# Retention and a mixture of adapters on one Trainium2 core: the rounds of a software pipeline in another order

## The chip, the core and the metric

The kernel runs on one core of a Trainium2 chip. The metric is the device time of one execution in microseconds (us). The kernel before takes 183.67 us, the median of three runs (182.58 to 185.34).

## What is computed

All arrays are fp32. q, k and v have 8 batches, 8 heads, 576 positions and 64 columns. The core of the reference, cut:

```python
scores = scale * np.matmul(q, k.transpose(0, 1, 3, 2))
gamma = 1.0 - 2.0 ** (-5.0 - np.arange(H, dtype=np.float32))
Dmat = np.where(rel >= 0, gamma[:, None, None] ** rel[None, :, :], 0.0)
attn = np.matmul(scores * Dmat, v)                # rel = i - j
x = attn.transpose(0, 2, 1, 3).reshape(B * S, H * D)      # 4608 x 512
logits = x @ w_gate                               # 8 experts
# the two largest logits, softmax over these two: weights w
delta[mask] += w * ((x[mask] @ A[e]) @ B[e])      # rank 16
out = x + delta
```

## The kernel before, in words

A *unit* is 128 positions of two batches with all their heads, so that there are four units for each of the four full chunks; the 64 positions that are left of each sequence make two short units of four batches each. `seq` (lines 142 to 144) lists the 18 units: 14 full ones (chunks 0, 1, 2 and half of chunk 3), a short one, two full ones, a short one. A retention over chunks needs a state P for each pair of batches, in SBUF, that is decayed and added to from chunk to chunk.

The kernel writes out the order of every engine's instructions by hand (`manual_schedule`, line 136), so each engine's queue is in program order. The loop over t (line 745) makes one round for each unit u = unit t, and does in it the late parts of p1 = unit t-1 and p2 = unit t-2. The stages on TensorE, with their matmuls for a full unit, are:

- T, `stage_T` (line 232): transposes of q (16) and of k (16) into PSUM, each tile of 64 rows by 128 columns of the array. VectorE (DVE) scales and copies q to qT; ScalarE (ACT) copies k to kT. `transposes` (line 622) makes both for unit t+1 and then has GpSimd (POOL) scale v and swap its halves.
- S, `stage_S` (274): scores of k and q, 64 matmuls in 64x64 tiles, into four banks; `mask` (299), four DVE multiplications, copies them to rt.
- Q, `stage_Q` (313): the state P times qT, 32 matmuls in 64x64 tiles, into the two banks of px. There is none for chunk 0.
- U, `stage_U` (328): the state product of v and k, 32 matmuls of 128 rows by 64 columns, into the bank pu. `state` (336): DVE adds P to it (ACT copies it for chunk 0), POOL decays the sum into P.
- R1 and R0, `stage_R1` (346) and `stage_R0` (360): late and early half of the retention, added into px; 32 matmuls each, R1 in tiles of 128x64 and R0 in tiles of 64x64. R1 of a unit is done in its own round, R0 in the next one, then `copy_x` has ACT copy px to xT.
- Z, `stage_Z`: xT times the joint matrix AW of gate and A, 16 matmuls of the full array, into the bank pz. `route1`, `sig`, `route2` find the two best experts and scale z to zc (nine small DVE steps, a sigmoid on ACT).
- X, `stage_X` (520): two fp16 transposes of zc into the bank pzt; ACT copies it to zT.
- B, `stage_B` (530): x is transposed back into the two banks of po by 16 matmuls in tiles of 64x128. Y, `stage_Y` (549): zT times Bcat is added to it, 4 fp16 matmuls. `evac` (555) has ACT copy po to osb, and `store` (563) issues two DMAs of 256 KB each.

A short unit has `short_S` (64 matmuls), `short_mask`, `short_Q` and `short_R` (64 matmuls each) and no state. `short_Q` ends with a small copy `seen`, for which `short_R` waits.

PSUM has eight banks, numbered by the tag; a stage says which it takes. In the kernel before, po has banks 2 and 3 and the pairs (4, 5) and (6, 7) swap roles each round: one holds S's first half and then px, the other X and Z. S's second half, pu and pt_k are in 0 and 1. The order of a full round on TensorE is

    B(p2) R0(p1) S(u) X(p2) Z(p1) Y(p2) Q(u) U(u) R1(u) T(t+1)

All loads and stores are issued by SyncE (SP), the loads of unit t+4 at the start of round t, the store of p2 later in it. Two rounds differ: those of the short units, and that of the full unit after a short one. After the loop `last_Z` and `finish` (line 631) end the last two units.

Of the kernel before, what the change touches and what calls it, by code (L numbers as in the profile page):

```python
# [10 lines left out]
FP32 = mybir.dt.float32  # L11
# [7 lines left out]
def kernel(  # L19
# [384 lines left out]
    def short_Q(u, bk):  # L404
# [12 lines left out]


        w = mo.tile([128, 1], FP32, tag="see", name="see")
        u.seen = nc.scalar.copy(out=w, in_=u.px[1][:, HP - 1, 1, 63:64])  # L420
# [19 lines left out]
    def copy_x(u, shared=False):  # L440
        u.xT = []
        for s in range(2):
# [8 lines left out]
    def stage_Z(u, bk):  # L451
        u.pz = bank(bk, [128, 2, ER + E], "pz")
        for s in range(2):
            for dt in range(HP):
                mm(u.pz[:, s, :], u.xT[s][:, dt, :], AW[s][:, dt, :], dt == 0, dt == HP - 1)


    def last_Z(u, p):
        u.pz = []
        for s in range(2):  # L460
            pz = bank(6 + s, [128, ER + E], "pz")
# [3 lines left out]
            if s == 0:  # L465
                stage_Y(p)

    def last_B(u):
        u.po = [
            [bank(2 + 2 * s + cc, [128, HP, 64], f"po{cc}") for cc in range(2)]  # L470
# [15 lines left out]
    def route1(u):  # L486
        lg = mo.tile([128, 2, E], FP32, tag="lg", name="lg")
        m8 = mo.tile([128, 2, E], FP32, tag="m8", name="m8")
        ns = mo.tile([128, 2], FP32, tag="ns", name="ns")
        ar = mo.tile([128, 2, E], FP32, tag="ar", name="ar")  # L490
        ge = mo.tile([128, 2, E], FP32, tag="ge", name="ge")
        nc.vector.tensor_copy(out=lg, in_=u.pz[:, :, ER : ER + E])  # L492
        for s in range(2):
            nc.vector.max(out=m8[:, s, :], in_=lg[:, s, :])
        nc.vector.tensor_tensor(out=ns, in0=m8[:, :, 0], in1=m8[:, :, 1], op=ALU.add)
        nc.vector.scalar_tensor_tensor(
            out=ar, in0=lg, scalar=2.0, in1=ns.unsqueeze(2).broadcast_to((128, 2, E)),
            op0=ALU.mult, op1=ALU.subtract,
        )
        nc.vector.tensor_tensor(  # L500
            out=ge, in0=lg, in1=m8[:, :, 1:2].broadcast_to((128, 2, E)), op=ALU.is_ge
        )
        u.ar, u.ge = ar, ge

    def sig(u):
        u.sg = mo.tile([128, 2, E], FP32, tag="sg", name="sg")
        nc.scalar.activation(out=u.sg, in_=u.ar, func=AFT.Sigmoid)

    def route2(u):
        cm = mo.tile([128, 2, E], FP32, tag="cm", name="cm")  # L510
        nc.vector.tensor_tensor(out=cm, in0=u.ge, in1=u.sg, op=ALU.mult)
        u.zc = mo.tile([128, 2, ER], FP16, tag="zc", name="zc", bufs=4)
        nc.vector.tensor_tensor(
            out=u.zc.rearrange("p s (e r) -> p s e r", e=E),
            in0=u.pz[:, :, 0:ER].rearrange("p s (e r) -> p s e r", e=E),
            in1=cm.unsqueeze(3).broadcast_to((128, 2, E, R)),
            op=ALU.mult,
        )

    def stage_X(u, bk):  # L520
        pzt = bank(bk, [128, 2, 128], "pzt", FP16)
        u.zT = mo.tile([128, 2, 128], FP16, tag="zT", name="zT")
        for s in range(2):
            nc.tensor.matmul(  # L524
                pzt[:, s, :], lhsT=u.zc[:, s, :], rhs=ident16,
                is_transpose=True, start=True, stop=True,
            )
# [27 lines left out]
    def evac(u, ccs):  # L555

        for cc in ccs:
# [3 lines left out]
            nc.scalar.copy(out=bass.AP(o.tensor, o.offset, ap), in_=u.po[cc])  # L561
# [60 lines left out]
    def transposes(i, bq):  # L622
        u = get(i)
        if u:
            stage_T(u, "q", bq)
            stage_T(u, "k", (0, 1))
            scale_v(u)

    def finish(u, p):
        m8 = mo.tile([128, 2, E], FP32, tag="m8", name="m8")
        ns = mo.tile([128, 2], FP32, tag="ns", name="ns")
        sg = mo.tile([128, 2, E], FP32, tag="sg", name="sg")
        cm = mo.tile([128, 2, E], FP32, tag="cm", name="cm")
        zc = mo.tile([128, 2, ER], FP16, tag="zc", name="zc", bufs=4)
        zT = mo.tile([128, 2, 128], FP16, tag="zT", name="zT")
        u.osb = osp.tile([128, 2, HP, 2, 64], FP32, tag="osb", name="osb", bufs=4)

        for s in range(2):  # L640
            lg = u.pz[s][:, ER : ER + E]
            nc.vector.max(out=m8[:, s, :], in_=lg)
            nc.vector.scalar_tensor_tensor(
                out=ns[:, s : s + 1], in0=m8[:, s, 0:1], scalar=-1.0, in1=m8[:, s, 1:2],
                op0=ALU.mult, op1=ALU.subtract,
            )
            nc.scalar.activation(
                out=sg[:, s, :], in_=lg, func=AFT.Sigmoid, scale=2.0, bias=ns[:, s : s + 1]
            )
            if s == 0:  # L650
                evac(p, [0, 1])
                store(p)
            nc.vector.scalar_tensor_tensor(
                out=cm[:, s, :], in0=lg, scalar=m8[:, s, 1:2], in1=sg[:, s, :],
                op0=ALU.is_ge, op1=ALU.mult,
            )
            nc.vector.tensor_tensor(
                out=zc[:, s, :].rearrange("p (e r) -> p e r", e=E),
                in0=u.pz[s][:, 0:ER].rearrange("p (e r) -> p e r", e=E),
                in1=cm[:, s, :].unsqueeze(2).broadcast_to((128, E, R)),  # L660
                op=ALU.mult,
            )
        for s in range(2):
            pzt = bank(6 + s, [128, 128], "pzt", FP16)
            nc.tensor.matmul(
                pzt, lhsT=zc[:, s, :], rhs=ident16, is_transpose=True, start=True, stop=True
            )
            nc.scalar.copy(out=zT[:, s, :], in_=pzt)
            if s == 0:
                last_B(u)  # L670
        for s in range(2):
            for cc in range(2):
                mm(u.po[s][cc], zT[:, s, :], bv[:, :, cc ^ s, :], False, True)
            for cc in range(2):
                o = u.osb[:, s, :, cc ^ s, :]
                if cc:
                    nc.vector.tensor_copy(out=o, in_=u.po[s][cc])
                else:
                    nc.scalar.copy(out=o, in_=u.po[s][cc])
            b0 = 4 * u.x + 2 * s  # L680
            nc.sync.dma_start(
                out=out3[b0 : b0 + 2, 128 * u.c : 128 * u.c + LH, :].rearrange("n t d -> t n d"),
                in_=u.osb[:, s].rearrange("p a o d -> p (a o d)"),
            )
# [41 lines left out]
    stage_U(u1, 3)  # L726
    state(u1)
    stage_R1(u1)
    route2(u0)
    transposes(2, (4, 5))  # L730


    def adapters(p1, p2, bd, late):
        stage_X(p2, bd[0])
        stage_Z(p1, bd[1])
        route1(p1)
        stage_Y(p2)
        evac(p2, [0])
        sig(p1)
        route2(p1)  # L740
        if not late:
            evac(p2, [1])
            store(p2)

    for t in range(2, NU):
# [3 lines left out]
        u, p1, p2 = get(t), get(t - 1), get(t - 2)  # L749
        ba, be = (0, 1), (2, 3)  # L750
        bc, bd = ((4, 5), (6, 7)) if t % 2 == 0 else ((6, 7), (4, 5))
        last = t == NU - 1
        stage_B(p2, be)
        if u.full and p1.full:
            stage_R0(p1, None if get(t - 2).full else p1.seen)
            copy_x(p1)
            stage_S(u, bc + ba)
            mask(u)
            adapters(p1, p2, bd, False)

            stage_Q(u, bc)
            stage_U(u, ba[0])
            state(u)
            stage_R1(u)
        elif u.full:

            adapters(p1, p2, bd, False)
            stage_S(u, bc + ba)
            mask(u)
            stage_U(u, bd[0])  # L770
            stage_Q(u, bc)
            state(u)
            stage_R1(u)
            u.seen = nc.scalar.copy(out=warm, in_=u.px[1][:, HP - 1, 127:128])
        else:
            stage_R0(p1)
            copy_x(p1)
            short_S(u, ba)
            short_mask(u)
            if last:  # L780
                short_Q(u, bc)
            adapters(p1, p2, bd, last)
            if not last:
                short_Q(u, bc)
            short_R(u)
            copy_x(u, last)
        transposes(t + 1, bd)
# [3 lines left out]
    evac(p2, [1])  # L791
    store(p2)
    stage_B(p1, (0, 1))
    stage_X(p1, 4)
    last_Z(u, p1)
    finish(u, p1)
    return


# [28 lines left out]
```

## Time and profile before

| What | Value |
|---|---|
| median of three runs | 183.67 us |
| the profiled execution | 183.51 us |
| its span, first to last instruction | 181.8 us |
| granted TensorE clock, mean | 0.998 |
| DMA | 38.85 MB, 214 GB/s |

The span is what the trace sees; the profiled execution's own time lies 1.7 us above it. In the profile PE is TensorE's matmuls and PEld its weight loads. A row of a group reads: line, engine, operation, output<-input by the program's names, shapes, count, busy time, mean ns of one. The helper `mm` (line 265) records most matmuls, so many groups have L266 and are told apart by their tiles. Rows of the stretches below have busy us and number of instructions of each engine, the granted clock, the DMA engines' busy share and GB/s.

### The profile page before, as it was taken

What the parts mean: (1) busy time and instruction counts of PE and PEld (TensorE: products, weight loads), DVE (VectorE), ACT (ScalarE), POOL (GpSimd) and SP (SyncE); (2) the same over time, 40 slices, a digit from 0 to 9 for tenths busy, and PEclk for the clock granted to TensorE, in tenths of its full rate; (3) what the DMA queues carried; (4) which work ended last, traced back from release to release, by engine and by line L of the source; (5) the groups of instructions that cost most, each with busy time, mean ns of one, the idle gap of its engine ahead of it and who ended that gap; (6) DMA issues with size and microseconds to landing.
All of it is one profiled execution on the core that took longest, in us unless ns stands there. A gap on an engine that the chain in (4) does not pass through costs nothing.

```text
span 181.8 us, 10235 instructions
## 1 busy us (share of the span) xinstructions
PE 172.1 (95%) x4636; PEld 155.9 (86%) x4636; DVE 95.4 (52%) x269; ACT 73.5 (40%) x160; POOL 81.6 (45%) x102
## 2 busy tenths in 40 slices
PE   7989999999999999999999999999998999799980
PEld 2779899999898989899999999988897899689960
DVE  1175754745564746555555555564654455445440
ACT  3236154545252525252534343433433632325450
POOL 7466582836271809090908181727258006316000
PEclk9999999999999999999999999999999999999999
DMA  5999999979899998998998899878999999820053
GB/s 134 273 231 215 234 234 233 203 180 230 194 227 271 251 225 208 217 257 209 253 243 208 227 223 271 199 212 202 270 213 281 230 248 239 322 94 34 5 215 133
DMA packets 119035, 38.85 MB, mean 214 GB/s; under 512 B 114248, under 2 KB 114376, under 8 KB 118992
## 3 DMA queue, kind: packets, MB, share of 16 engines
q1 hardware_dynamic: 118688, 38.04, 84.1%
q8 instruction: 36, 0.59, 1.3%
q0 software_dynamic: 144, 0.13, 0.5%
q14 instruction: 7, 0.06, 0.1%
q10 hardware_dynamic: 160, 0.03, 0.1%
HBM read 28.88 MB, written 9.44 MB: 211 GB/s over the span
## 4 chain that ended last, share of the span: by engine, by line
PE 91%; DVE 3%; issue 2%; ACT 0%; DVEq 0%; ACTq 0%
PE px L266 23%; PE pz L266 19%; PE ps L266 12%; PE pu L266 9%; PE pt_q L240 6%; PE pt_k L240 5%; PE po L536 5%; PE po L266 4%; PE fill L266 3%; PE pzt L524 2%; PE ps_s L266 1%; DVE rt L305 1%; PE pa L266 1%; PE pl L266 1%; DVE qT L252 0%
## 5 line engine op out<-in xcount | busy, mean ns | idle before, releaser
L344 POOL TENSOR_TENSOR P<-pn,gdec 128x512 f32<-128x512 f32 x16 | 20.4, 1274 | 76.9 <-DVE pn L341 66.1
L305 DVE TENSOR_TENSOR rt<-ps,tri 128x384 f32<-128x384 f32 x64 | 31.3, 550 | 17.2 <-PE ps L266 17.2
L266 PE MATMUL pz<-AW,xT 128*128 128x136 f32 x288 | 37.8, 283 | 0.5 <-issue 0.5
L212 POOL TENSOR_TENSOR v<-v,pack 128x512 f32<-128x512 f32 x35 | 35.8, 1043 | 5.1 <-DMA v<-in_v_dram 5.0
L262 ACT COPY kT<-pt_k 128x512 f32<-128x512 f32 x36 | 19.3, 589 | 40.6 <-PE pt_k L240 40.6
L266 PEld LDWEIGHTS pz<-AW,xT 128*128 128x128 f32 x288 | 34.7, 190 | 0.9 <-issue 0.7
L252 DVE TENSOR_TENSOR qT<-pt_q,aqp 128x512 f32<-128x512 f32 x36 | 23.2, 686 | 23.1 <-PE pt_q L240 23.1
L561 ACT COPY osb<-po 128x512 f32<-128x512 f32 x34 | 19.5, 577 | 29.7 <-PE po L266 26.0
L266 PE MATMUL ps<-qT,kT 64*64 64x128 f32 (+1 forms) x1024 | 26.1, 247 | 1.7 <-issue 1.2
L266 PEld LDWEIGHTS ps<-qT,kT 64*64 64x64 f32 x1024 | 24.1, 133 | 2.8 <-issue 1.5
L266 PE MATMUL px<-rt,v 64*64 64x64 f32 (+1 forms) x512 | 21.5, 224 | 0.1
L266 PE MATMUL px<-rt,vs 64*64 64x64 f32 (+1 forms) x512 | 21.2, 223 | 0.0
L223 POOL COPY vs<-v 64x512 f32<-64x512 f32 x32 | 19.8, 618 | 1.7
L448 ACT COPY xT<-px 128x512 f32<-128x512 f32 x34 | 18.5, 593 | 3.4 <-PE px L266 2.6
L266 PEld LDWEIGHTS px<-rt,v 64*64 64x64 f32 (+1 forms) x512 | 17.8, 136 | 1.7 <-DVE rt L305 0.3
L266 PE MATMUL pu<-v,k 128*64 128x64 f32 x512 | 18.4, 225 | 0.1
L266 PEld LDWEIGHTS pu<-v,k 128*64 128x64 f32 x512 | 16.2, 138 | 2.7 <-issue 2.3
L266 PEld LDWEIGHTS px<-rt,vs 64*64 64x64 f32 (+1 forms) x512 | 17.6, 136 | 0.0
L266 PE MATMUL px<-qT,P 64*64 64x128 f32 (+1 forms) x512 | 15.6, 262 | 0.1
L266 PEld LDWEIGHTS px<-qT,P 64*64 64x64 f32 x512 | 12.5, 133 | 2.8 <-DVE lg L492 2.1
L341 DVE TENSOR_TENSOR pn<-pu,P 128x512 f32<-128x512 f32 x12 | 8.3, 691 | 9.1 <-PE pu L266 9.1
L240 PE MATMUL pt_q<-id,q 64*128 64x64 f32 x288 | 12.8, 229 | 0.0
(69 smaller groups left out, 164.7 us busy)
## 6 DMA issues: line engine op xcount, KB each, us to landing
q<-in_q_dram SPq DMA_DIRECT2D x36, 256.0 KB, 5.0
k<-in_k_dram SPq DMA_DIRECT2D x36, 256.0 KB, 4.5
v<-in_v_dram SPq DMA_DIRECT2D x36, 256.0 KB, 4.8
out_dram<-osb SPq DMA_DIRECT2D x36, 256.0 KB, 4.4
A<-in_moe_A_dram SPq DMA_DIRECT2D x1, 256.0 KB, 3.8
Bcat<-in_moe_B_dram POOLq DMA_DIRECT2D x1, 128.0 KB, 4.5
g<-c_g ACTq DMA_DIRECT2D x1, 20.0 KB
pack<-c_rest ACTq DMA_DIRECT2D x1, 10.0 KB, 2.9
```

The source lines that it names most:

```text
L212: eng.tensor_tensor(out=u.v[:, b * H : b * H + H, :], in0=u.v[:, b * H : b * H + H, :], in1=(gv if u.full else gvh).unsqueeze(2).broadcast ...
L223: nc.gpsimd.tensor_copy(out=vs[half(1 - r)], in_=u.v[half(r), H : 2 * H, :])
L240: nc.tensor.matmul(ps[r][:, hp, b, :], lhsT=src[sl, b * H + 2 * hp : b * H + 2 * hp + 2, :], rhs=id64[sl, :], is_transpose=True, start=Tru ...
L252: u.scaled = nc.vector.tensor_tensor(out=o, in0=ps[r], in1=aqp[:, :, a0 : a0 + 64].unsqueeze(2).broadcast_to((128, HP, 2, 64)), op=ALU.mult,)
L262: nc.scalar.copy(out=o, in_=ps[r])
L266: return nc.tensor.matmul(o, lhsT=l, rhs=r, start=start, stop=stop, skip_group_check=True)
L305: nc.vector.tensor_tensor(out=r.rearrange("p a s i -> p a (s i)"), in0=u.ps[ho][g].rearrange("p a s i -> p a (s i)"), in1=tri3.rearrange(" ...
L341: u.sum = nc.vector.tensor_tensor(out=flat(pn), in0=flat(u.pu), in1=flat(P[u.bp]), op=ALU.add)
L344: nc.gpsimd.tensor_tensor(out=flat(P[u.bp]), in0=flat(pn), in1=flat(gdec), op=ALU.mult)
L448: nc.scalar.copy(out=o, in_=u.px[s])
L536: nc.tensor.matmul(po[cc][:, s, dt, :], lhsT=u.xT[s][sl, dt, :], rhs=id64[sl, :], is_transpose=True, start=(dt == 0 and s == 0), stop=Fals ...
L561: nc.scalar.copy(out=bass.AP(o.tensor, o.offset, ap), in_=u.po[cc])
```

## The change

From t=5 on (`t > TURN`) a full round on TensorE is

    S(u) Z(p2) Y(p3) R0(p1) Q(u) T(t+1) B(p2) U(u) R1(u) X(p2)

so the adapters run one round later than before: Z in round t is that of unit t-2, and Y, evac and store are those of p3 = unit t-3. Rounds 2 and 3 keep the old order, round 4 has neither Z nor Y, and the end has more of them. Three pairs of banks turn: S's first half is in the pair a, which then takes Z (one bank for each half of pz) ; its second half is in c, which then takes px (in round 4, Q takes a instead); T writes to a[1], d[0] for q and d[1], a[0] for k, where d holds px of p1. U then takes a[1] and X takes d[0]. The three pairs then change roles. The routing is done half by half (eight DVE steps, two sigmoids). X is done in half columns, four matmuls in place of two, where it follows R1. The diff, cut to its core:

```diff
-    def stage_Z(u, bk):
-        u.pz = bank(bk, [128, 2, ER + E], "pz")
+    def stage_Z(u, bks, ss=(0, 1)):
+        if 0 in ss:
+            u.pz = []
+        for s in ss:
+            pz = bank(bks[s], [128, ER + E], "pz")
             for dt in range(HP):
                 mm(pz, u.xT[s][:, dt, :], AW[s][:, dt, :], dt == 0, dt == HP - 1)
             u.pz.append(pz)
...
+    def route(u):
...
+        def best(s):
+            nc.vector.max(out=m8[:, s, :], in_=lg[s])
+            nc.vector.scalar_tensor_tensor(
+                out=ns[:, s : s + 1], in0=m8[:, s, 0:1], scalar=-1.0, in1=m8[:, s, 1:2],
+                op0=ALU.mult, op1=ALU.subtract,
+            )
+            nc.scalar.activation(
+                out=sg[:, s, :], in_=lg[s], func=AFT.Sigmoid, scale=2.0, bias=ns[:, s : s + 1]
+            )
+
+        def times(s):
+            nc.vector.scalar_tensor_tensor(
+                out=cm[:, s, :], in0=lg[s], scalar=m8[:, s, 1:2], in1=sg[:, s, :],
+                op0=ALU.is_ge, op1=ALU.mult,
+            )
+            nc.vector.tensor_tensor(
...
         for s in range(2):
+            best(s)
+        for s in range(2):
+            times(s)
...
+    def stage_X(u, bk, cols=True):
...
+            for r in (half(0), half(1)) if cols else (slice(0, 128),):
+                nc.tensor.matmul(
+                    pzt[r, s, :], lhsT=u.zc[:, s, r], rhs=ident16,
+                    is_transpose=True, start=True, stop=True,
+                )
...
     stage_T(u1, "k", (0, 1))
+    stage_Z(u0, (2, 3))
     scale_v(u1)
...
-    stage_Z(u0, 2)
-    route1(u0)
-    sig(u0)
+    route(u0)
     stage_S(u1, (6, 7, 0, 1))
     mask(u1)
...
-    route2(u0)
-    transposes(2, (4, 5))
+    transposes(2, (4, 5), (0, 1))
...
+    TURN = 4
+    a, c, d, e = (0, 1), (4, 5), (6, 7), (2, 3)
     for t in range(2, NU):
...
+        u, p1, p2, p3 = get(t), get(t - 1), get(t - 2), get(t - 3)
         last = t == NU - 1
+        if t <= TURN:
+            stage_B(p2, e)
+            stage_R0(p1)
             copy_x(p1)
+        if t < TURN:
...
+        if u.full:
+            stage_S(u, a + c)
             mask(u)
+        else:
+            short_S(u, c)
+            short_mask(u)
+        if t > TURN:
+            stage_Z(p2, a)
+            route(p2)
+            stage_Y(p3)
+            evac(p3, [0])
+            if p1.full:
+                stage_R0(p1)
+                copy_x(p1)
+            evac(p3, [1])
+            store(p3)
+        if t == TURN:
+            stage_Q(u, a)
+            x, y, d = d, c, a
+        else:
+            if u.full:
+                stage_Q(u, c)
+            else:
+                short_Q(u, c, nc.vector.tensor_copy if last else nc.scalar.copy)
+            x, y, d = (a[1], d[0]), (d[1], a[0]), c
+        transposes(t + 1, x, y)
+        if last:
+            stage_X(p2, x[1])
+            short_R(u)
+            copy_x(u, True)
+        if t > TURN:
+            stage_B(p2, e)
+        if last:
+            stage_B(p1, a)
+            break
+        if u.full:
+            stage_U(u, x[0])
             state(u)
             stage_R1(u)
         else:
+            short_R(u)
+            copy_x(u, True)
+        stage_X(p2, x[1], u.full)
+        a, c = y, x
...
+    d0, d1 = x[1], y[0]
+    stage_Z(p1, (d1, c[0]))
+    route(p1)
+    stage_Y(p2)
+    evac(p2, [0, 1])
     store(p2)
+    stage_Z(u, (d0, c[1]), [0])
+    stage_X(p1, d1, False)
+    stage_Z(u, (d0, c[1]), [1])
+    route(u)
+    last_B(u, e + (c[0], d1))
...
+    last_X(0, nc.scalar.copy)
+    stage_Y(p1)
+    evac(p1, [0])
+    last_X(1, nc.vector.tensor_copy)
+    evac(p1, [1], nc.vector.tensor_copy)
+    store(p1)
...
```

The last unit's four products Y, its copies by ACT and DVE and its two stores follow as before.

More of the change, by code (lines that the diff above doesn't have):

```diff
@@ L402, in short_mask, with short_Q @@
             u.rt.append(r)
-    def short_Q(u, bk):
+    def short_Q(u, bk, copy=nc.scalar.copy):
         u.px = [bank(bk[s], [128, HP, 2, 64], f"px{s}") for s in range(2)]
@@ L419, in short_Q @@
         w = mo.tile([128, 1], FP32, tag="see", name="see")
-        u.seen = nc.scalar.copy(out=w, in_=u.px[1][:, HP - 1, 1, 63:64])
+        u.seen = copy(out=w, in_=u.px[1][:, HP - 1, 1, 63:64])
     def short_R(u):
@@ L437, in short_R, with copy_x @@
                             first = False
-    def copy_x(u, shared=False):
-        u.xT = []
-        for s in range(2):
+    def copy_x(u, shared=False, ss=(0, 1)):
+        if 0 in ss:
+            u.xT = []
+        for s in ss:
             xt = mo.tile([128, HP, 128], FP32, tag="xT", name="xT", bufs=8)
@@ L449, in copy_x @@
             u.xT.append(xt)
-    def stage_Z(u, bk):
-        u.pz = bank(bk, [128, 2, ER + E], "pz")
[L453 to L461, printed above, removed]
+    def stage_Z(u, bks, ss=(0, 1)):
+        if 0 in ss:
+            u.pz = []
+        for s in ss:
+            pz = bank(bks[s], [128, ER + E], "pz")
             for dt in range(HP):
@@ L464, in last_Z, with last_B @@
             u.pz.append(pz)
-            if s == 0:
-                stage_Y(p)
-    def last_B(u):
+    def last_B(u, bks):
         u.po = [
-            [bank(2 + 2 * s + cc, [128, HP, 64], f"po{cc}") for cc in range(2)]
+            [bank(bks[2 * s + cc], [128, HP, 64], f"po{cc}") for cc in range(2)]
             for s in range(2)
@@ L484, in last_B @@
                     )
-    def route1(u):
-        lg = mo.tile([128, 2, E], FP32, tag="lg", name="lg")
+    def route(u):
         m8 = mo.tile([128, 2, E], FP32, tag="m8", name="m8")
         ns = mo.tile([128, 2], FP32, tag="ns", name="ns")
-        ar = mo.tile([128, 2, E], FP32, tag="ar", name="ar")
-        ge = mo.tile([128, 2, E], FP32, tag="ge", name="ge")
-        nc.vector.tensor_copy(out=lg, in_=u.pz[:, :, ER : ER + E])
-        for s in range(2):
[L494 to L518, printed above, removed]
@@ L520, in stage_X @@
-    def stage_X(u, bk):
+        sg = mo.tile([128, 2, E], FP32, tag="sg", name="sg")
+        cm = mo.tile([128, 2, E], FP32, tag="cm", name="cm")
+        u.zc = mo.tile([128, 2, ER], FP16, tag="zc", name="zc", bufs=4)
+        lg = [u.pz[s][:, ER : ER + E] for s in range(2)]
+        def best(s):
[7 more added lines that the diff above has]
+            )
@@ new lines, in times @@
+        def times(s):
[4 more added lines that the diff above has]
+            nc.vector.tensor_tensor(
+                out=u.zc[:, s, :].rearrange("p (e r) -> p e r", e=E),
+                in0=u.pz[s][:, 0:ER].rearrange("p (e r) -> p e r", e=E),
+                in1=cm[:, s, :].unsqueeze(2).broadcast_to((128, E, R)),
+                op=ALU.mult,
+            )
@@ L523, in stage_X @@
         for s in range(2):
[L524 to L527, printed above, removed]
+            for r in (half(0), half(1)) if cols else (slice(0, 128),):
+                nc.tensor.matmul(
+                    pzt[r, s, :], lhsT=u.zc[:, s, r], rhs=ident16,
+                    is_transpose=True, start=True, stop=True,
+                )
         nc.scalar.copy(out=u.zT, in_=pzt)
@@ L553, in stage_Y, with evac @@
         u.osb = osp.tile([128, 2, HP, 2, 64], FP32, tag="osb", name="osb", bufs=4)
-    def evac(u, ccs):
+    def evac(u, ccs, copy=nc.scalar.copy):
         for cc in ccs:
@@ L560, in evac @@
             ap[1][0] += -64 if cc else 64
-            nc.scalar.copy(out=bass.AP(o.tensor, o.offset, ap), in_=u.po[cc])
+            copy(out=bass.AP(o.tensor, o.offset, ap), in_=u.po[cc])
     def store(u):
@@ L620, in get, with transposes @@
         return G.get(i)
-    def transposes(i, bq):
+    def transposes(i, bq, bk):
         u = get(i)
@@ L625, in transposes @@
             stage_T(u, "q", bq)
-            stage_T(u, "k", (0, 1))
+            stage_T(u, "k", bk)
             scale_v(u)
[L631 to L684, printed above, removed]
@@ L725 @@
     stage_Q(u1, (6, 7))
-    stage_U(u1, 3)
+    stage_U(u1, 4)
     state(u1)
     stage_R1(u1)
-    route2(u0)
-    transposes(2, (4, 5))
[L733 to L743, printed above, removed]
+    transposes(2, (4, 5), (0, 1))
+    TURN = 4
+    a, c, d, e = (0, 1), (4, 5), (6, 7), (2, 3)
     for t in range(2, NU):
@@ L748 @@
             G[t + 4] = make(t + 4)
-        u, p1, p2 = get(t), get(t - 1), get(t - 2)
-        ba, be = (0, 1), (2, 3)
-        bc, bd = ((4, 5), (6, 7)) if t % 2 == 0 else ((6, 7), (4, 5))
+        u, p1, p2, p3 = get(t), get(t - 1), get(t - 2), get(t - 3)
         last = t == NU - 1
-        stage_B(p2, be)
-        if u.full and p1.full:
-            stage_R0(p1, None if get(t - 2).full else p1.seen)
+        if t <= TURN:
+            stage_B(p2, e)
+            stage_R0(p1)
             copy_x(p1)
-            stage_S(u, bc + ba)
+        if t < TURN:
+            stage_S(u, c + a)
@@ L758 @@
             mask(u)
-            adapters(p1, p2, bd, False)
-            stage_Q(u, bc)
-            stage_U(u, ba[0])
+            stage_X(p2, d[0], False)
+            stage_Z(p1, (d[1], c[1]))
+            route(p1)
+            stage_Y(p2)
+            evac(p2, [0, 1])
+            store(p2)
+            stage_Q(u, c)
+            stage_U(u, a[0])
             state(u)
             stage_R1(u)
-        elif u.full:
-            adapters(p1, p2, bd, False)
-            stage_S(u, bc + ba)
-            mask(u)
-            stage_U(u, bd[0])
-            stage_Q(u, bc)
+            transposes(t + 1, d, a)
@@ new lines @@
+            c, d = d, c
+            continue
+        if u.full:
+            stage_S(u, a + c)
+            mask(u)
+        else:
[16 more added lines that the diff above has]
+            if u.full:
+                stage_Q(u, c)
+            else:
+                short_Q(u, c, nc.vector.tensor_copy if last else nc.scalar.copy)
+            x, y, d = (a[1], d[0]), (d[1], a[0]), c
@@ L772 @@
+        transposes(t + 1, x, y)
[10 more added lines that the diff above has]
+            stage_U(u, x[0])
             state(u)
             stage_R1(u)
-            u.seen = nc.scalar.copy(out=warm, in_=u.px[1][:, HP - 1, 127:128])
         else:
-            stage_R0(p1)
-            copy_x(p1)
-            short_S(u, ba)
@@ L779 @@
[L779 to L784, printed above, removed]
             short_R(u)
-            copy_x(u, last)
-        transposes(t + 1, bd)
+            copy_x(u, True)
+        stage_X(p2, x[1], u.full)
+        a, c = y, x
     u, p1, p2 = get(NU - 1), get(NU - 2), get(NU - 3)
-    evac(p2, [1])
-    store(p2)
-    stage_B(p1, (0, 1))
-    stage_X(p1, 4)
-    last_Z(u, p1)
@@ L796, with last_X @@
-    finish(u, p1)
+    d0, d1 = x[1], y[0]
+    stage_Z(p1, (d1, c[0]))
+    route(p1)
+    stage_Y(p2)
+    evac(p2, [0, 1])
+    store(p2)
+    stage_Z(u, (d0, c[1]), [0])
[3 more added lines that the diff above has]
+    last_B(u, e + (c[0], d1))
+    zT = mo.tile([128, 2, 128], FP16, tag="zT", name="zT")
+    def last_X(s, copy):
+        pzt = bank((d0, c[1])[s], [128, 128], "pzt", FP16)
+        nc.tensor.matmul(
+            pzt, lhsT=u.zc[:, s, :], rhs=ident16, is_transpose=True, start=True, stop=True
+        )
+        copy(out=zT[:, s, :], in_=pzt)
@@ new lines @@
+    last_X(0, nc.scalar.copy)
[4 more added lines that the diff above has]
+    store(p1)
+    u.osb = osp.tile([128, 2, HP, 2, 64], FP32, tag="osb", name="osb", bufs=4)
+    for s in range(2):
+        for cc in range(2):
+            mm(u.po[s][cc], zT[:, s, :], bv[:, :, cc ^ s, :], False, True)
+        for cc in range(2):
+            o = u.osb[:, s, :, cc ^ s, :]
+            if cc:
+                nc.vector.tensor_copy(out=o, in_=u.po[s][cc])
+            else:
+                nc.scalar.copy(out=o, in_=u.po[s][cc])
+        b0 = 4 * u.x + 2 * s
+        nc.sync.dma_start(
+            out=out3[b0 : b0 + 2, 128 * u.c : 128 * u.c + LH, :].rearrange("n t d -> t n d"),
+            in_=u.osb[:, s].rearrange("p a o d -> p (a o d)"),
+        )
```

## The prediction

> **What bounds the kernel now.** I read the page first: parts 1 and 4 say that TensorE is busy nearly all the time and carries the chain that ended last.
>
> ```profile
> PE 172.1 (95%) x4636; PEld 155.9 (86%) x4636; DVE 95.4 (52%) x269; ACT 73.5 (40%) x160; POOL 81.6 (45%) x102
> ```
> ```profile
> PE 91%; DVE 3%; issue 2%; ACT 0%; DVEq 0%; ACTq 0%
> ```
>
> A busy PE can still be a PE that waits, so I cut one steady round (t=8) at the first matmul of each stage. In order: S, X, Z, Y, Q, U, R1, both transposes T, B, R0.
>
> ```profile
> core 0: us, PE busy (x) PEld busy (x) DVE busy (x) ACT busy (x) POOL busy (x), PEclk, DMA share, GB/s
> 79.47:80.97 1.50, 1.50 (x76) 1.43 (x69) 0.54 (x2) 1.22 (x3) 1.44 (x3) 1.00 1.09 246
> 80.97:81.09 0.12, 0.12 (x8) 0.12 (x3) 0.12 (x2) 0.00 (x0) 0.12 (x1) 1.00 1.27 335
> 81.10:83.00 1.90, 1.90 (x18) 1.89 (x17) 1.28 (x3) 0.37 (x1) 0.84 (x2) 1.00 1.08 344
> 83.00:83.53 0.53, 0.53 (x6) 0.29 (x3) 0.29 (x3) 0.00 (x0) 0.00 (x0) 1.00 1.17 259
> 83.53:84.57 1.04, 1.04 (x34) 0.86 (x33) 0.71 (x6) 1.00 (x3) 0.00 (x0) 1.00 1.04 244
> 84.57:85.55 0.98, 0.98 (x36) 0.98 (x34) 0.43 (x2) 0.27 (x1) 0.00 (x0) 1.00 0.18 41
> 85.55:86.58 1.03, 1.03 (x38) 0.96 (x34) 0.69 (x1) 0.00 (x0) 0.00 (x0) 1.00 0.80 186
> 86.58:87.64 1.06, 1.06 (x36) 1.06 (x34) 0.30 (x1) 0.00 (x0) 0.96 (x1) 1.00 0.83 183
> 87.64:88.24 0.60, 0.60 (x22) 0.53 (x18) 0.60 (x2) 0.40 (x1) 0.60 (x2) 1.00 1.15 262
> 88.24:88.77 0.53, 0.53 (x36) 0.53 (x33) 0.38 (x1) 0.53 (x2) 0.53 (x1) 1.00 0.86 193
> ```
>
> The reader sees no gap: 9.30 us per round, and rounds 8 to 11 all take 9.30. No new order can win by hiding waits there; it can only change what lies between stages. The losses are elsewhere. The timeline shows stalls of 0.1 to 0.2 us in S at t=3 to 7, 0.18 and 0.53 at t=12, 0.74 and 0.50 at t=14, 1.6 at t=16 and 0.3 at t=17. The chain of waits at t=16:
>
> ```profile
> 154.49 1.27 PE ps L266 x53
> 155.76 1.22 issue
> 156.97 0.55 PE ps L266 x9
> ```
>
> Nothing that the program waits for stands there. Counting PE's records (loads, matmuls and its semaphore instructions), the stalls at 125.4, 138.4, 157.0 and 166.4 us all come at number 193 or 194 modulo 256, and the 36 packets of the instruction queue have 16 KB each. They are refills of the instruction stream: from a packet's start to the next block's first instruction 2.2 to 2.6 us pass when PE waits. All stalls at this remainder sum to 3.9 us; without them the span is 177.9.
>
> **What the Trainium skill says.** "Runtime: NRT & Kernel Launch", Instruction fetch mechanics: instructions come in 16 KiB blocks of 256, and a crossing is "mostly hidden". The trace has the blocks but not the hiding. "TensorEngine Tiling (Array Packing)", Key Properties: changing the tiling mode drains the engine. The trace agrees: the 16 matmuls of q's transpose right after R1 (another mode) take 0.55, those of k's after them 0.51; B before R0 (another mode) takes 0.60 against 0.50. A change costs 0.10 ahead of it and up to 0.05 after it. "PSUM — Partial Sum Buffer", PSUM bank collisions: guard by bank, so a matmul into a bank waits for its last reader; the new bank table is read by that rule.
>
> **The change, part by part.** Mode changes first. Old: S-X, Y-Q, Q-U, R1-T, B-R0. New: S-Z, Y-R0, Q-T, B-U, X-S. Five each, so the new order saves none.
>
> *Regular full round (t=5 to 13, 16).* S 1.50, then Z into the first bank of S, which waits for the first mask. The mask starts 0.96 after S and takes 0.55, 0.05 to be seen: 1.57 instead of 1.50. Z right after a change 1.91+0.05=1.96. Y 0.53, R0 0.53, Q 1.03 (0.98 if it gains from no longer following a change; R0 ahead of it is of its own mode), T 1.06, B 0.60, U 0.98. R1 loses the change behind it: 0.93. X as four half-column matmuls: not in the old trace; between 0.12 (free beside R1) and 0.35 (four of the 0.067 steps of the old pair, then 0.15 to leave); I take 0.07+0.15=0.22. Sum 9.41, +0.11 (between 9.26 and 9.6 with these ends).
>
> The shorter routing, eight small DVE steps and two sigmoids for nine steps and one, lies under PE's work (DVE is busy 0.52 of the span) and costs nothing there; it counts where zc is waited for, below.
>
> Covers in that round: q's transposes need the bank of copy_x (ACT order sig, sig, evac, copy, copy, evac): from Y's start ACT ends the first copy_x about 0.06 before T_q, the second 0.1 before T_k, the second evac 0.13 before B. DVE's zc is ready at 5.2, T_q starts at 5.6. All fit, none with room: if ACT is late, PE waits. POOL: scale_v and swap of t+1 (3.3 us) now stand before the P update, which is next needed four rounds on. SP: the store moves one round later, so from unit 9 on loads pass two more DMAs (about 1.3 us of queue earlier).
>
> *Prologue.* route(u0) has its last steps before mask(u1) on DVE. From pz at 18.90: 0.21+0.28+0.30+0.26+0.29 (steps of the old tail's chain) = 20.24, against 19.94: +0.3. t=2 therefore starts at 24.13. t=2 and 3 keep their order, 8.26 and 8.40: 40.79.
>
> *t=4.* B 0.60, R0 0.53, then S; Q takes S's first two banks and waits for two masks, 2.00 from S's start. Q 1.03, T 0.55+0.60, U waits for qT out of its bank: T_q's start +0.75+0.69+0.06=1.50, 0.35 late; U 0.98, R1 0.93, X 0.22. Sum 7.79: 48.58. Its Z and Y are paid at the end. Nine rounds: 133.27.
>
> *t=14 (short).* short_S takes the bank of X, just issued: X to zT copied is 0.75 in the old trace, so it starts 0.6 late. 0.60+1.29+1.96+0.53+0.53+1.09+1.06+0.60+1.09+0.22=8.97: 142.24. The old wait on `seen` (0.50) is gone, covered by T and B. *t=15:* no R0, so T waits 0.15 for zc: 9.03. *t=16:* 9.41: 160.68.
>
> *End, from there (t=17).* B of this round goes behind short_R. short_S late again, 0.60+1.29=1.89, Z 1.96, Y 0.53, R0 0.53, Q to short_R 1.59 (the old 0.65 wait on `seen` stays, X within it), short_R 1.09, two B 1.15, Z 1.96, Y 0.44, half Z 0.93, X late by 0.35 and 0.12, half Z 0.93: 13.5. Then a chain: pz seen 0.35 after its last matmul, routing 1.37, X, zT on DVE, evac of p1 on DVE 0.68, done at 16.5. SP then issues four stores (0.34, 0.43, 0.55, 0.55 in the old tail), the last at 17.95; from its issue to the end of the program the old trace has 3.89. Sum 21.84: span 182.5 without refills. Old: 3.9 of 181.8 are refills. For the new I take 2.6, fewer because its own waits (about 3 us) give the fetch time; 128 matmuls take between 3.6 and 5.6 us in both orders, so they don't vanish: 0.5 to 5. Span 185.1. The profiled run took 183.51, 1.7 over its span, and the median is 183.67: I add 1.7 and get 186.8.
>
> **Rivals.** *Refills fall into waits* (0.5 instead of 2.6): 184.7, not slower as far as a measurement can tell. For it: rounds 8 to 11 lost nothing. Against it: the dense stretch (R1, X, S) is as short as the old (B, R0, S). It decides once the new order's refills stay under 1 us. *ACT becomes the bound of the regular round:* the margins above are 0.06 to 0.13; with ACT 0.3 late PE loses 0.2 in each of ten rounds: 188.8. For it: five copies in a row; against it: each length is from a row. *Loads late:* T now comes some 4 us earlier against DMA, which carries 38 MB at a share near 1. k of unit 5 is issued by 40.0 and lands 3.9 to 5.6 later, T_k is due at 45.5: at worst some 1 us there and at t=5: 187.8. *The order does save:* X is free, Z and the masks cost nothing (9.2 a round), refills 0.5, t=4 without its waits: 182.5-2.1-1.0+0.5+1.7, about 181.6; with the tail 2 us better, under 180.
>
> **How the numbers follow.** My case 0.55 (its own range 185.2 to 188.4), refills 0.18, ACT 0.16, loads 0.07, saving 0.04. The range 183.8 to 189.6 leaves out the saving and the outer halves of the refill and ACT cases. Two per cent, about what a measurement of this kernel can tell from no change, is 180.0 to 187.3: a third of my case, the ACT case and the loads give slower 0.40; faster 0.04; within 0.56.
>
> **What would show it.** Regular rounds of 9.4 with Z about 1.57 after S; `ps_s` twice 0.6 late behind ACT's zT; Q at t=4 waiting for rt; idle PE without a releaser only at the 194th of 256 instructions; the last store 18 us after the last short_S was due. Rounds at 9.3 or below, or a tail under 20 us, would prove the costs wrong; rounds over 9.6, the margins.

## The result, and the profile after

The changed kernel takes 190.14 us (median of 6 runs, 188.62 to 194.11) against 184.84 (6 runs, 182.58 to 188.24, the three of above among them) for the kernel before: ratio 1.0347, 95% interval 1.0244 to 1.0451. Ratios and intervals compare only the faster executions of each kernel, those within 1.5% of its fastest, while medians are of all. It is slower, as the forecast leaned, but by twice as much (186.8 is 1.7% over the 183.67 that the forecast started from), and outside the range (183.8 to 189.6). The profiled execution took 190.78 us, its span is 189.1; the span's difference to before is 7.3 us.

Parts 1 and 4 of the page after. TensorE's share has hardly moved, but the chain now holds DVE at 6% and ACT at 3%, where they had 3 and 0:

```profile
PE 176.2 (93%) x4662; PEld 157.1 (83%) x4662; DVE 102.7 (54%) x273; ACT 74.5 (39%) x172; POOL 82.0 (43%) x102
```
```profile
PE 85%; DVE 6%; issue 3%; ACT 3%; DVEq 0%; ACTq 0%
```

A regular round of the new order without a stall, cut like the old one; in order S, Z, Y, R0, Q, both T, B, U, R1, X:

```profile
100.92:102.50 1.58, 1.57 (x69) 1.43 (x65) 0.61 (x2) 0.37 (x1) 1.58 (x2) 1.00 0.98 224
102.50:104.45 1.95, 1.95 (x16) 1.94 (x17) 1.66 (x5) 0.14 (x1) 1.89 (x3) 1.00 1.05 240
104.45:104.98 0.53, 0.53 (x6) 0.29 (x3) 0.29 (x3) 0.13 (x1) 0.49 (x2) 1.00 1.24 272
104.98:105.50 0.52, 0.52 (x33) 0.52 (x36) 0.49 (x4) 0.38 (x2) 0.52 (x1) 1.00 1.18 261
105.50:106.49 0.99, 0.99 (x46) 0.82 (x38) 0.44 (x2) 0.99 (x3) 0.01 (x1) 1.00 0.56 128
106.49:107.54 1.05, 1.05 (x36) 1.05 (x34) 0.30 (x1) 0.84 (x2) 0.00 (x0) 1.00 1.21 341
107.54:108.15 0.61, 0.61 (x23) 0.54 (x19) 0.61 (x2) 0.41 (x1) 0.00 (x0) 1.00 1.04 350
108.15:109.13 0.98, 0.98 (x35) 0.98 (x34) 0.38 (x1) 0.67 (x2) 0.00 (x0) 1.00 0.99 219
109.13:110.06 0.93, 0.93 (x38) 0.93 (x36) 0.64 (x1) 0.00 (x0) 0.00 (x0) 1.00 1.20 265
110.06:110.28 0.22, 0.22 (x11) 0.13 (x7) 0.05 (x1) 0.00 (x0) 0.02 (x1) 1.00 1.30 284
```

This is t=10. It takes 9.35 us, against 9.30 before and 9.41 forecast; from S to Z pass 1.58, and X takes 0.22. But only two of the rounds t=5 to 13 (t=5 is the other) are that clean. The nine took 89.6 us, 5.4 more than nine times 9.35. Two kinds of gaps fill the difference.

**The first kind is a refill**, as before. The chain of waits at t=8, S broken off seven matmuls before its end:

```profile
79.89 1.43 PE ps L266 x57
81.33 1.34 issue
82.67 0.34 PE ps L266 x7
```

Counted in all traces in one way (from one matmul's start to the next, where that is over 0.13 us and takes in a record 191 to 197 modulo 256, less 0.06), refills cost 3.8 us before and 5.1 after.

**The second kind was not foreseen.** The timeline of t=7 on all engines, lines on the path alone:

```profile
start us, us, engine line op out<-in xcount [idle before <-releaser]
...
73.43 0.17 DVE L492 MAX8 m<-pz 128x8 f32<-128x8 f32 x1 [0.54 <-PE pz L266]
73.61 1.04 POOL L212 TENSOR_TENSOR v<-v,pack 128x512 f32<-128x512 f32 x1 [2.46 <-DMA v<-in_v_dram]
73.64 1.02 DVE L493 SCALAR_TENSOR_TENSOR ns<-m 128x1 f32<-128x1 f32 x1
...
74.76 0.27 ACT L497 ACTIVATE sg<-pz,ns 128x8 f32<-128x8 f32 x1 [1.49 <-DVE ns L493]
...
74.93 0.58 ACT L561 COPY osb<-po 128x512 f32<-128x512 f32 x1
...
75.32 0.29 DVE L506 TENSOR_TENSOR zc<-pz,cm 128x128 f16<-128x128 f32 x1
75.39 1.09 ACT L449 COPY xT<-px 128x512 f32<-128x512 f32 x2
...
75.71 0.24 PE L240 MATMUL pt_q<-id,q 64*128 64x64 f32 x1 [0.38 <-issue]
```

`ns` is one element per partition and takes 0.16 us. Here it takes 1.02 and ends when POOL's v-scaling ends, which began 0.03 earlier. Behind it come, on DVE, the rest of the routing up to zc, and on ACT, in order, the sigmoid, the evac and the two copies of px. T of q needs the bank of Z's second half, which zc reads last, and then a bank of px, which ACT's first copy reads: from one matmul's start to the next 0.65 and then 0.33 us pass, where the clean round has 0.20 at the first of these places and no gap at the second. The groups of `ns`, before and then after:

```profile
L495 DVE TENSOR_TENSOR ns<-m 128x2 f32<-128x2 f32 x17 | 3.1, 180 | 0.6
```
```profile
L493 DVE SCALAR_TENSOR_TENSOR ns<-m 128x1 f32<-128x1 f32 x36 | 10.4, 288 | 1.2
```

The mean of 288 ns is made of values from 0.16 to 0.25 us and of eight from 0.42 to 1.02; most of T's late starts (t=7, 8, 11, 14) follow one of the eight. Before, `ns` was no smaller a risk by its operands, but in the regular rounds POOL was idle then. (In the prologue it was held there too: 0.35 us in this trace, 0.87 in a second one.) Round t=8 before, POOL and `ns`:

```profile
78.61 2.04 POOL L212 TENSOR_TENSOR v<-v,pack 128x512 f32<-128x512 f32 x2
80.72 1.26 POOL L223 COPY vs<-v 64x512 f32<-64x512 f32 x2
83.68 0.16 DVE L495 TENSOR_TENSOR ns<-m 128x2 f32<-128x2 f32 x1
86.68 1.27 POOL L344 TENSOR_TENSOR P<-pn,gdec 128x512 f32<-128x512 f32 x1 [4.70 <-DVE pn L341]
```

There the scaling follows T at the round's end and is over at 82, 1.7 us before `ns`. In the new order T is earlier, the scaling waits for v, and it falls on the routing. The waits of POOL for v (us in sum, times, longest), before and then after:

```profile
POOL v L212 <- DMA v<-in_v_dram: 5.0, 4, 2.3
```
```profile
POOL v L212 <- DMA v<-in_v_dram: 24.1, 12, 3.5
```

The Trainium skill has the mechanism ("SBUF — State Buffer", Who interferes with whom: a DVE instruction with two SBUF inputs contends with a GpSimd instruction that reads SBUF). `ns` reads m8 twice, and this trace agrees; `cm`, with one SBUF tensor and one in PSUM, keeps 0.21 to 0.23 us throughout.

### The profile page after: what moved, and what is told of

Its sections match the earlier page's. It is cut to its first block, busy times and chain, and to the rows that moved or that the text cites. A ratio compares the mean times of both kernels' runs of the same rounds, so it can differ in the third digit from the quotient of the medians.

```text
span 189.1 us, 10292 instructions
## 1 busy us (share of the span) xinstructions
PE 176.2 (93%) x4662; PEld 157.1 (83%) x4662; DVE 102.7 (54%) x273; ACT 74.5 (39%) x172; POOL 82.0 (43%) x102
## 4 chain that ended last, share of the span: by engine, by line
PE 85%; DVE 6%; issue 3%; ACT 3%; DVEq 0%; ACTq 0%
PE pz L266 19%; PE px L266 19%; PE ps L266 12%; PE pu L266 9%; PE pt_q L240 6%; PE po L536 5%; PE pt_k L240 4%; PE po L266 3%; PE fill L266 3%; DVE ns L493 2%; PE pzt L524 1%; DVE rt L305 1%; PE ps_s L266 1%; ACT osb L561 1%; ACT xT L449 1%
## 5 line engine op out<-in xcount | busy, mean ns | idle before, releaser
L497 ACT ACTIVATE sg<-pz,ns 128x8 f32<-128x8 f32 x36 | 9.6, 268 | 58.4 <-DVE ns L493 54.1
L266 PE MATMUL ps<-qT,kT 64*64 64x128 f32 (+1 forms) x1024 | 26.9, 248 | 3.0 <-issue 2.5
L266 PE MATMUL px<-rt,v 64*64 64x64 f32 (+1 forms) x512 | 22.1, 224 | 0.2
L528 ACT COPY zT<-pzt 128x256 f16<-128x256 f16 x17 | 6.4, 375 | 22.1 <-PE pzt L524 22.1
L240 PE MATMUL pt_q<-id,q 64*128 64x64 f32 x288 | 14.1, 229 | 1.1 <-issue 0.4
```

The costliest lines, as they stand in the source:

```text
L240: nc.tensor.matmul(ps[r][:, hp, b, :], lhsT=src[sl, b * H + 2 * hp : b * H + 2 * hp + 2, :], rhs=id64[sl, :], is_transpose=True, start=Tru ...
L266: return nc.tensor.matmul(o, lhsT=l, rhs=r, start=start, stop=stop, skip_group_check=True)
L497: nc.scalar.activation(out=sg[:, s, :], in_=lg[s], func=AFT.Sigmoid, scale=2.0, bias=ns[:, s : s + 1])
```

## Experiments

Theory A: the blocked `ns` is a cause of its own. Theory B: only TensorE's structure (order, end) costs, and A's stalls merely take the place of refills. Theory C: refills stop TensorE because the fetch stands in a DMA queue behind loads. Theory D, formed later: where the 256-record blocks end in the round decides how much.

**1. `ns` with one tensor input** (changed kernel; value unchanged).

```diff
-            nc.vector.scalar_tensor_tensor(
-                out=ns[:, s : s + 1], in0=m8[:, s, 0:1], scalar=-1.0, in1=m8[:, s, 1:2],
+            nc.vector.tensor_scalar(
+                out=ns[:, s : s + 1], in0=m8[:, s, 0:1], scalar1=-1.0, scalar2=m8[:, s, 1:2],
```

> The changed kernel, in which the small step ns = -(m0+m1) is a tensor_scalar with the second maximum as a per-partition scalar, so that it has one tensor input in SBUF instead of two. Theory A (POOL's scaling of v now runs at the time of the routing and blocks ns, which makes ACT's sigmoid, evac and copy_x late, and so TensorE's transposes): ns takes 0.2 us everywhere also while POOL works (up to 1.0 us in the changed kernel), the late starts of 0.27 and 0.45 us in the transposes of q at t=7, 8, 11, 14 go, and the kernel is 1.5 to 2.2 us faster than the changed kernel, about 1.024 of before. Theory B (the loss is only in bank waits and instruction refills): ns may be short, but the time stays within 0.5 us of the changed kernel, 1.035 of before.

189.21 us (4 runs), ratio to before 1.0117 (0.9957 to 1.0277). Its timeline shows a full overlap without effect:

```profile
91.24 0.21 DVE L493 TENSOR_SCALAR ns<-m 128x1 f32<-128x1 f32 x1
91.45 1.04 POOL L212 TENSOR_TENSOR v<-v,pack 128x512 f32<-128x512 f32 x1 [1.98 <-DMA v<-in_v_dram]
92.17 0.21 DVE L493 TENSOR_SCALAR ns<-m 128x1 f32<-128x1 f32 x1
```
```profile
L493 DVE TENSOR_SCALAR ns<-m 128x1 f32<-128x1 f32 x36 | 7.7, 214 | 1.3
```

All 36 take 0.21 to 0.22 us and T's stalls behind px are gone, though POOL waited 56.6 us for v in this run. So the second SBUF tensor is what is blocked, and not the kind of step: `cm` is a SCALAR_TENSOR_TENSOR like the old `ns`. The interval is too wide to price it, so both were run again in one job:

> The changed kernel once more, beside the run with the one-input ns on the same chip: 188 to 191.5 us, 2.5 to 4.5% over the kernel before; ns over 400 ns at least three times, and T late behind copy_x or zc each time.

> The changed kernel with ns as a step with one tensor input, once more, beside the changed kernel itself. If the blocked ns is what made the regular rounds uneven, it is 1 to 2.5 us (0.6 to 1.3%) faster than the changed kernel in the same job. If its stalls only took the place of refills, the two are within 0.4%.

The changed kernel gave 189.41 us, 1.0271 (1.0208 to 1.0335), with five `ns` of 0.48 to 1.03; only two rounds had T late behind them. The one-input form gave 189.28 us, 1.0175 (1.0062 to 1.0287), again with none. The ratios lie 0.96% apart here and 2.3% in the two jobs before, in line with A, but the intervals overlap. The mechanism is shown in the traces. Its price is not settled: Q and T together, over their undisturbed 2.04 us (2.10 in a short round), lose 2.1 us behind long `ns` in the first trace of the changed kernel and only about 0.8 in the second.

**2. Old rounds up to t=11** (`TURN = 12`; Z and U take banks free in the old order).

```diff
-    TURN = 4
+    TURN = 12
...
-            stage_Z(p1, (d[1], c[1]))
+            stage_Z(p1, (d[1], a[0]))
...
-            stage_U(u, a[0])
+            stage_U(u, a[1])
```

> The changed kernel with TURN = 12 instead of 4: rounds 2 to 11 keep the order of before, only with the new routing (the second half of Z goes to bank a[0], pu to a[1]); rounds 12 to 17 and the end are those of the change. If the order of the regular rounds is what costs (0.05 us of bank and mode waits each, and the routing under POOL's scaling of v): rounds 5 to 11 take 9.30 instead of 9.35 plus stalls of the transposes, 2 us less in all, about 1.02 of before. If only the new end, the short rounds and the refills cost: within 0.7 us of the changed kernel, 1.03 or more of before.

188.71 us, 1.0195 (1.0094 to 1.0296). Rounds 5 to 11 take 9.30 to 9.82 again; two blocked `ns` of 0.87 and 0.88 come in the first rounds of the new order, and refills cost 5.2. About half of the loss stays, as far as the intervals tell. It does not need the new rounds 5 to 11: it lies in the prologue, the transition and the end, and 1.0 to 1.4 us of it are refills over the kernel before's.

**3 and 4. A third of the loads,** in the kernel before and in the changed one (later units use the tiles of units 0 to 5, so the output is that of other data, and POOL's step multiplies v by ones).

```diff
     def load(i):
+        if i >= 6:
+            nat[i] = nat[i - 6]
+            return
...
-                in1=(gv if u.full else gvh).unsqueeze(2).broadcast_to((128, H, Dh)),
+                in1=(gv if u.i < 6 else ones[:, 0:H]).unsqueeze(2).broadcast_to((128, H, Dh)),
```

> The kernel before, but only the first six of 18 units load q, k and v; the later ones take the tiles of the unit six before (v is then multiplied by ones), so the output is that of other data. Theory C (refills of TensorE's instructions are late because the DMA queues are full of loads): the stalls at the 194th of 256 instructions go, 3.5 to 4 us in all, about 0.98 of before. Rival (a refill takes 2.4 us whatever else moves): the stalls stay, within 1 us of before.

> The changed kernel with the same third of its loads, other data in later units. Theory C: its refill stalls go too, 4.5 us or more, to about 1.005 to 1.01 of before; what is left over the kernel before with a third of its loads, some 4 to 5 us, is the price of the order, the routing under POOL and the end. Rival (refills do not depend on the DMA load): stays at 1.03.

The kernel before: 181.17 us, 0.9769 (0.9665 to 0.9873). The changed one: 186.01 us, 1.0056 (1.0025 to 1.0087). The DMA part of the page, before and with a third of the loads:

```profile
q1 hardware_dynamic: 118688, 38.04, 84.1%
```
```profile
q1 hardware_dynamic: 43808, 19.16, 37.7%
```

Refills fell to 2.5 us in both, in the first most of it while the loads still ran. In the trace, the refill's packet starts 1.6 us on average after the previous block's end is passed in the kernel before (21 blocks between 55 and 150 us), and 0.30 with a third of the loads; from its start to the next block's first instruction 2.2 to 2.6 us pass when TensorE waits. So C holds as far as the fetch goes: with the loads it starts later, and TensorE loses time without any wait that the program knows. That it stands in a queue behind them is inferred. And C explains a part only: the ratio 0.9769 is 4.3 us, more than the 1.3 to 1.7 by which the refills fell (from 3.8 and 4.2) and the 1.5 between the two profiled executions; the rest shows in no trace. The stalls did not all go, as C had expected.

The quotient 1.0056/0.9769 = 1.029, 5.3 us (about 3.3 to 7.3 by the two intervals; the two spans, 185.1 and 180.3, differ by 4.8), is the price of order and end where refills are alike and no `ns` takes over 0.47 us. T of k in the prologue, which waits 1.34 us for its load in the trace of the changed kernel and 0.40 in the other, is in it. B's structure is real and the larger part.

**5. The two short rounds' pairs exchanged**, on the base of experiment 4.

```diff
         else:
+            a, c = c, a
             short_S(u, c)
```

> The changed kernel with the loads of units 0 to 5 alone (the later units take the same tiles, so their data are other ones), and in the two short rounds the pairs a and c exchanged before short_S, so that it goes to the pair that X did not just use. The wait of 0.48 us of short_S behind ACT's zT goes twice: 184.1 to 185.3 us, 0.4 to 0.6% below the 186.0 of the same kernel without the exchange, unless Z then waits for zT or for the U bank, in which case the time stays.

184.28 us, 0.9989 (0.9960 to 1.0018), 0.7% below experiment 4: both waits of short_S for zT went, and nothing took their place. This line of the waits is in the changed kernel and not here:

```profile
PE ps_s L266 <- ACT zT L528: 0.5, 2, 0.3
```

**6. Both repairs with all loads** (edits of 1 and 5 together).

> The changed kernel with all loads and both repairs: ns with one tensor input, and the pairs a and c exchanged before short_S. Against the changed kernel (1.027 and 1.035 times the kernel before in two jobs) it loses the T stalls behind ns and 2 x 0.48 us: 1.010 to 1.018 times before, 187 to 188.5 us. If the structure of the new order and its end is the rest (about 4 us, less what the exchange gave), it stays above before; a ratio under 1.005 would say that the two repairs were nearly all of the loss.

190.54 us beside 188.85 for the kernel before on that chip, 1.0111 (0.9944 to 1.0277): the ratio is within the expectation, the time is not, and neither is better than experiment 1's as far as the interval tells. In its trace both repairs are there; refills cost 5.8, and T of k waited for its load, 1.71 us of it at t=4, after which the granted clock stood at 0.50 from 49.5 to 52.9 us:

```profile
PE pt_k L240 <- DMA k<-in_k_dram: 2.0, 3, 1.5
```

No version found beats the kernel before.

**7. The kernel before with its instructions shifted.** Nothing of the rounds is changed; a filler of the prologue is replaced by tiny matmuls, so that the blocks end elsewhere.

```diff
-    filler(7, 1, 256)
+    for _ in range(18):
+        mm(bank(7, [128, 4, 128], "fill")[0:64, 0, 0:16], ones[0:64, 0:64], ones[0:64, 0:16], True, True)
```

> The kernel before with one filler of 256 columns in the prologue's idle time replaced by 18 tiny matmuls, so that every later PE instruction stands about 64 records further in its stream. If the stalls without a releaser are refills of the instruction stream, they stay at records 193 to 195 modulo 256 and so move to other stages of the rounds, some 64 records earlier in the order (a third of a round); their sum lies between 2 and 5.5 us, and the time within 1.5% of before's. If they belong to places in the program (S at t=16, Z at t=14), they stay at those places and their records become 1 to 3 modulo 256.

Each tiny matmul waited for the one before (0.34 us each, 6.3 in all), which spoils the time: 190.75 to 195.59 us, at a lower granted clock (0.977 in the profile, where it stood at 0.50 from 13.7 to 20.5 us), so no ratio is given. But the stalls moved as the refill theory says: they stay at records 192 to 195 modulo 256, now in T of k, Z, R, Q and B as well as S. They cost 9.0 us, well over the expected 2 to 5.5. With one tile for all of them:

```diff
-    filler(7, 1, 256)
+    fl = bank(7, [128, 512], "fill")
+    for i in range(18):
+        mm(fl[0:64, 16 * i : 16 * i + 16], ones[0:64, 0:64], ones[0:64, 0:16], True, True)
```

> The shift of about 64 records once more, with the 18 tiny matmuls in one tile of the bank, so that none waits for another: they should take under 1 us. If the position of the instruction blocks in the round decides how long refills stop TensorE, the stalls at records 193 to 195 modulo 256 sum to 7 us or more, as in the first shift (9.0 us against 3.8 in the kernel before), and the time is 2 to 3% over before's. If the 9.0 was chance, the sum is 3 to 5.5 and the time within 1%.

> 27 tiny matmuls, a shift of about 100 records. The same two theories: if the position decides, the sum differs from 3.8 us by 2 us or more in either direction and the time by 1% or more; if it does not, the sum is 3 to 5.5 us and the time within 1%. In both the stalls stay at records 193 to 195 modulo 256.

> The kernel before as one of the runs, for a second trace of it on this chip: within 1% of itself, refill stalls of 3 to 5 us in sum, regular rounds of 9.30 us.

The shift of 64: 187.1 to 190.6 us, median 188.91 against 185.87, 1.6% more where 2 to 3 was expected; refills 8.1 us. The shift of 100 (`range(27)`): 191.80 us, 1.0356 (1.0107 to 1.0606); refills 9.8. The kernel before itself: 1.0043 (0.9998 to 1.0087), refills 4.2. The tiny matmuls themselves lengthen the prologue by 1.0 and 2.0 us (T of unit 0 to T of unit 1 takes 8.21 and 9.26, not 7.26; with the shift of 64, T of unit 0 began 1.1 us earlier). Against the first trace of the kernel before, refills grew by 4.3 and 6.0 us and the spans (185.3 and 189.0) by 3.5 and 7.2, so most of the loss is refills. The chain of the shift of 100 shows t=9 to 11, which had no gap in the kernel before:

```profile
92.48 1.39 PE ps L266 x59
93.87 1.05 issue
94.92 0.34 PE ps L266 x5
...
103.15 1.26 PE ps L266 x51
104.41 1.08 issue
105.50 0.55 PE ps L266 x9
...
113.95 1.06 PE ps L266 x42
115.00 1.01 issue
116.01 0.67 PE ps L266 x16
```

The break moves 8 or 9 matmuls earlier each round, as the blocks do, and costs 1.0 us or a little more each time. So D holds: the 256 records that end in S after T, B and R0 are many short instructions and pass in 3.2 to 3.5 us, while the fetch starts 1.75 to 2.5 us late and needs 2.25 more. In rounds 8 to 11 of the kernel before the blocks end in U, R0, Q and B, take 3.7 to 5.3 us, and hide it. None of the three shifts lowered the sum: the kernel before owes its low sum to where its blocks happen to end.

## Why the prediction was wrong

It had the sign and most of the structure. Against its span of 185.1 the trace has 189.1; the 4.0 us are +2.5 refills (5.1 for 2.6), +2.1 late T behind blocked `ns` (t=7, 8, 11 and 14), +0.8 start, -1.0 end, -0.4 the rest. Its term for the structure, 182.5 - 177.9 = 4.6 us, is near what experiments 3 and 4 price. Of the absolute miss, 190.14 for 186.8, 1.2 us lie in the kernel before, whose median rose from 183.67 to 184.84; the spans have no part in that.

- **Five mode changes before and after, so no saving:** the stretches agree. No stretch of the regular round differs from its term by more than 0.05.
- **Regular round 9.41:** 9.35 measured. Only Q was over-priced, at 1.03 for 0.99.
- **t=4, 7.79:** 8.17, with both waits in their places: Q 0.30 behind the masks, U 0.59 behind qT, where 0.35 was forecast.
- **t=14 and 15, 8.97 and 9.03:** 9.61 and 9.08. short_S waited 0.48 (forecast 0.6) behind zT; the surplus of t=14 is T behind a blocked `ns`.
- **End 21.84:** 20.85. Its `seen` wait was put at 0.65 and was 0.27; the other 0.6 is not taken apart here.
- **Prologue, t=2 at 24.13:** 25.16. Of the 1.03, 0.26 is the first load (T of unit 0 began that much later), 0.25 a refill in T of unit 1 (counted above), 0.29 is R1, which waited 0.59 longer than before for its masks where 0.3 was forecast: `ns` again, 0.82 and 0.55 us, ahead of them on DVE. The last 0.2 is not taken apart.
- **Failed step: "POOL: scale_v and swap of t+1 (3.3 us) now stand before the P update, which is next needed four rounds on."** It asked who waits for POOL's result and not who shares its port while it runs, and so put the routing at nothing for the regular round ("costs nothing there"). So "DVE's zc is ready at 5.2" and the ACT margins of 0.06 to 0.13 rested on a routing at its undisturbed length. The rival of a late ACT had the symptom (T late, some 0.3 us) and the wrong cause: ACT's copies kept their length and started late. What the traces showed in its place is an `ns` of up to 1.02 us for 0.16, and 2.1 us of late T (about 0.8 in the second trace); in the two traces of experiment 1 it is gone. (The old routing has eight DVE steps like the new one, not nine; nothing hangs on that.)
- **Failed step: refills "I take 2.6, fewer because its own waits (about 3 us) give the fetch time".** The trace has 5.1. Waits help only inside a block that is short, and the new waits lie elsewhere. That the blocks' place sets the sum was not seen; the rival of refills at 0.5 fails with it. Two traces of each kernel give 3.8 and 4.2 before, 5.1 and 4.9 after, but the one-input form, with the same PE instructions, gives 3.0 and 5.1, so the 1 us between the orders is within their scatter. Shifts alone moved the sum in the kernel before from 3.8 to 9.8: it belongs to the place of the code, not to the idea of the change.
- **Loads late, 0.07:** it came in other traces. In the five traces of the new rounds from t=5 on with all loads, T of k at t=4 stood 1.35, 1.39 and 1.71 us in three; in the one shown above it did not. Its chance of 0.07 was for the whole loss, but as a term of it the rival was right.

What stays open: the exact price of the blocked `ns` in time, since the intervals overlap, how much of the loss is refills, what a third of the loads saves beyond the refills, and why the fetch's delay varies between 0 and 3 us from block to block under the same load.

## What to carry to other kernels

When a change moves work of GpSimd in time, look at which small DVE steps with two SBUF tensors it now overlaps, and what queues behind them in order; a pointer as the second operand removes the risk for 0.05 us. In a kernel of thousands of short PE instructions, find the records at which blocks end and see whether the 256 ahead of each take longer than the fetch; the sum can move by several us through edits that have nothing to do with the rounds, so a ratio of 1 or 2% between two orders may be only that (a shift alone gave 1.6 and 3.6%). An order that adds no work and hides every wait can still lose by its ends: here they and the transition were most of a structural 5 us.

## What the runs showed of the hardware

- A one-element DVE step with two SBUF inputs was held for as long as a GpSimd step of 1.04 us ran (1.02); with one tensor and a pointer it took 0.21 in full overlap.
- A refill of PE's instructions starts 0.30 us on average after the previous block's end is passed where loads are few, and 1.6 us after it among all loads; from its packet's start to the next block's first instruction it takes 2.2 to 2.6 us. The Trainium skill ("Runtime: NRT & Kernel Launch", Instruction fetch mechanics) says that the next page is fetched while the current one runs; the traces agree, and a block that passes in less than the delay plus 2.2 us then stops TensorE, in single cases by up to 2.0 us.
- Cutting the loads to a third, none of which TensorE waited for in the rounds, made the kernel before 2.3% faster (1.0 to 3.4); refills account for 1.3 to 1.7 of these 4.3 us.
